# Attention results held by feature, with the exponentials divided before they are turned, in a fused attention and gated-MLP kernel

## The chip, the cores and the metric

The kernel runs on one core of one Trainium2 chip. The metric is device microseconds (us) for one execution. Engines are named as in the profile: PE (TensorE, matrix multiply), PEld (its weight loads), DVE (VectorE), ACT (ScalarE), POOL (GpSimd), SP (SyncE, here an issuer of DMAs). SBUF is the on-chip working memory, PSUM the accumulator memory that PE writes, in banks of 512 float32 per partition.

## The reference, cut to what matters

```python
# q, k, v: (8 batches, 8 heads, 576 positions, 64)
scores = q @ k.T / 8
mask   = heads 0..3: the last 32 positions;  heads 4..7: every 4th of the last 128
attn   = exp(scores - max);  attn = attn / (attn.sum() + 1e-9)
x      = (attn @ v) as (4608 tokens, 512 features)
g, val = x @ w_gate, x @ w_val          # 512 -> 1536
out    = (g * sigmoid(g) * val) @ w_out # 1536 -> 512
```

Attention is sparse: each query sees 32 keys. The MLP over 4608 tokens is nearly all of the arithmetic.

## The kernel before, in words

**The MLP.** It works on transposed tokens (features on partitions). Each float32 operand is split into a high part and a remainder, and three products stand for one full-precision product; these are the `128x512` multiplies of lines 515, 552 and 841 in the profile, 3564 of them. The first three chunks of 512 tokens are computed plainly (lines 515 and 552). Meanwhile the weights are converted, and in the third chunk also mixed (lines 719 to 732) into "pieces" that are written to memory. The last three chunks of 1024 tokens use a Strassen-like scheme with seven products (line 841), whose weights come back as pieces through POOL's DMA queue (line 770), and whose intermediate sums and splits are made by DVE (line 804) and ACT (lines 831 and 846).

**The attention.** It is cut into 46 packs. A pack is a pair of heads over a stretch of tokens, in groups of four blocks of 32 queries; a block has 64 keys, and 32 of them count for each query. Packs of pairs 0 and 1 have the plain mask, those of pairs 2 and 3 the dilated one, where a block takes every fourth position. Packs 0 to 3 are done at the start, before any MLP work, with helpers of their own (`first_...`). The 42 packs from number 4 on have 2, 3 or 4 groups, 136 in all, and are threaded into the MLP's stream of multiplies at fixed slots: `attend` is called after each slot, and a table gives each pack m a slot A and a slot B, three or six slots later.

- At A(m): `results` of pack m-1 (line 457), then `scores` of pack m (line 417), both on PE into the two banks of the PSUM tile `two`, head 0 in bank 0 and head 1 in bank 1. DVE then runs `norm` of m-1 (lines 466 to 468): it adds a small number to the sum of exponentials, which an extra column of ones in v has produced, takes the reciprocal and multiplies it onto the results, queries on partitions. Then `shift` of m (lines 429, 431, 432: add the mask, take the maximum, subtract it) and `exps` on ACT (line 437). Loads of v and of the next q and k are issued from ACT.
- At B(m): `turn_y` transposes the normed results of m-1 on PE (line 475), so that features stand on partitions. `turn_e` transposes the exponentials of m (line 441), so that keys stand on partitions, and `keys` copies them to SBUF (line 447). `x_copies` writes the transposed results into the MLP's x (line 497 for the last three chunks, lines 488 and 489 for chunks 1 and 2, which need the high part and the remainder).

In `results` a block of exponentials, turned, is the stationary operand: 64 keys by 32 queries, so that eight such tiles fit on the 128 by 128 array (2 row halves by 4 column quarters). The values, 64 features and the column of ones, are streamed through, 65 columns. In `scores` the stationary operand is 64 features by 32 queries, and 64 keys are streamed. A multiply of these two kinds leaves two records in the trace; the program's order shows it once.

**What sets the order.** The start is written out by hand. After it the Tile framework's scheduler places instructions on each engine in the order in which its own model of the program finds them ready, so a row can stand earlier or later than the code says. Each engine works through its own order strictly.

## Time and profile before

| what | value |
|---|---|
| median of 3 runs | 935.71 us (935.17 to 936.23) |
| the profiled execution, own time | 934.96 us |
| its span, first to last instruction | 933.2 us |
| granted TensorE clock | 1.0 |
| PE busy | 921.8 us (99%) |
| DVE, ACT, POOL busy | 639.2, 391.1, 253.8 us |
| bytes moved by DMA | 205.45 MB, 220 GB/s on average |

A row of the timeline reads: start, duration (both us), engine, line, operation, output<-inputs, array tile (rows*columns), shape, count, and in brackets the idle time of the engine before it with what ended it. A row of the groups gives busy time, mean ns of one instruction, and idle time before them. Durations on PE overlap: a `128x512` multiply is shown with some 0.39 us, but starts follow each other every 0.227 us, so costs on PE are read from starts.

### The profile page before, as it was taken

How to read it: one execution, taken by the hardware profiler on the slowest of the kernel's cores; microseconds unless marked ns; L12 is line 12 of the kernel's file. 1: busy time of each engine (PE TensorE's matmuls, PEld its weight loads, DVE VectorE, ACT ScalarE, POOL GpSimd, SP SyncE). 2: the span in 40 equal slices, each digit the busy share in tenths (PEclk: the TensorE clock that was granted, in tenths of full speed). 3: DMA queues.
4: the chain of work that ended last, by engine and by line, in shares of the span. 5: the costliest groups of instructions: out<-in, count | busy, mean ns of one | idle time of the engine just before them, and what ended most of it. 6: DMA issues, size and time to landing. Idle time of an engine off the chain costs nothing.

```text
span 933.2 us, 20559 instructions
## 1 busy us (share of the span) xinstructions
PE 921.8 (99%) x8499; PEld 751.5 (81%) x8499; DVE 639.2 (68%) x1055; ACT 391.1 (42%) x664; POOL 253.8 (27%) x307
## 2 busy tenths in 40 slices
PE   7999999999999999999999999999999999999998
PEld 4778788878888878888888888888888888888886
DVE  6764738668678775757669965666689745656863
ACT  4865623323334233343345643343355523334351
POOL 6655421111111212133223111222223112343320
PEclk9999999999999999999999999999999999999999
DMA  9974515667786980767777778766766686656663
GB/s 349 349 255 174 175 41 198 235 205 262 245 287 217 305 307 5 267 217 222 226 226 236 239 224 255 242 217 213 247 208 195 219 255 189 195 189 195 201 207 111
DMA packets 75533, 205.45 MB, mean 220 GB/s; under 512 B 7728, under 2 KB 22320, under 8 KB 75440
## 3 DMA queue, kind: packets, MB, share of 16 engines
q0 software_dynamic: 27728, 100.77, 34.6%
q1 hardware_dynamic: 35472, 65.16, 19.7%
q10 hardware_dynamic: 12240, 38.20, 11.9%
q8 instruction: 67, 1.10, 0.5%
q14 instruction: 26, 0.21, 0.1%
HBM read 161.64 MB, written 42.47 MB: 219 GB/s over the span
## 4 chain that ended last, share of the span: by engine, by line
PE 73%; DVE 3%; DMA 1%; issue 1%; ACT 1%; SPq 0%; ACTq 0%; DVEq 0%
PE bo L841 32%; PE bv L841 12%; PE bg L841 12%; PE bo L552 4%; PE bg L515 4%; PE bv L515 4%; PE two L457 2%; PE two L417 2%; DMA pieces<-at_float32r 1%; PE two L441 1%; PE two L475 1%; DVE at_float32r L732 0%; SPq L740 0%; DVE at_float L529 0%; DVE at_float L719 0%
## 5 line engine op out<-in xcount | busy, mean ns | idle before, releaser
L841 PE MATMUL bo<-at_float32r 128*128 128x512 f32 x1296 | 307.1, 390 | 0.0
L841 PEld LDWEIGHTS bo<-at_float32r 128*128 128x128 f32 x1296 | 242.2, 188 | 50.6
L770 POOL DMA_DIRECT2D at_float32r<-pieces x189 | 101.3, 536 | 376.7 <-PE bo L841 216.6
L804 DVE TENSOR_TENSOR at_float<-bo,at_float 128x512 f32<-128x512 f32 (+1 forms) x169 | 114.2, 684 | 104.9 <-ACT at_float L846 49.5
L804 DVE TENSOR_TENSOR at_float32r<-at_float,at_float32r 128x512 fp32r<-128x512 f32 (+1 forms) x147 | 114.0, 800 | 40.0 <-ACT at_float32r L831 27.1
L841 PE MATMUL bv<-at_float32r 128*128 128x512 f32 x486 | 129.5, 393 | 0.0
L841 PE MATMUL bg<-at_float32r 128*128 128x512 f32 x486 | 129.3, 392 | 0.0
L515 PE MATMUL bg<-at_float32r,at_float32r 128*128 128x512 f32 x432 | 106.7, 394 | 0.8 <-DVE at_float32r L505 0.4
L515 PE MATMUL bv<-at_float32r,at_float32r 128*128 128x512 f32 x432 | 107.1, 394 | 0.0
L552 PE MATMUL bo<-at_float32r,at_float32r 128*128 128x512 f32 x432 | 106.2, 394 | 0.0
L841 PEld LDWEIGHTS bv<-at_float32r 128*128 128x128 f32 x486 | 90.2, 188 | 19.0
L841 PEld LDWEIGHTS bg<-at_float32r 128*128 128x128 f32 x486 | 90.3, 188 | 18.8
L831 ACT CAST at_float32r<-at_float 128x512 fp32r<-128x512 f32 x126 | 77.0, 622 | 67.4 <-PE bv L841 21.3
L544 POOL TENSOR_TENSOR at_float32r<-at_float,at_float32r 128x512 fp32r<-128x512 f32 x36 | 48.6, 1351 | 204.8 <-PE bo L552 138.3
L515 PEld LDWEIGHTS bg<-at_float32r,at_float32r 128*128 128x128 f32 x432 | 79.9, 188 | 18.8 <-DVE at_float32r L505 1.2
L515 PEld LDWEIGHTS bv<-at_float32r,at_float32r 128*128 128x128 f32 x432 | 79.7, 188 | 17.1 <-DVE at_float L534 0.4
L552 PEld LDWEIGHTS bo<-at_float32r,at_float32r 128*128 128x128 f32 x432 | 79.7, 188 | 16.9
L867 ACT ACTIVATE at_float<-at_float 128x512 f32<-128x512 f32 x72 | 45.6, 633 | 81.7 <-DVE at_float L804 81.7
L846 ACT COPY at_float<-bg 128x512 f32<-128x512 f32 x63 | 37.0, 587 | 94.2 <-PE bg L841 94.0
L529 DVE SCALAR_TENSOR_TENSOR at_float<-at_float,bg 128x512 f32<-128x512 f32 x36 | 24.7, 686 | 66.9 <-ACT at_float L524 66.9
L279 POOL TENSOR_TENSOR at_float32r<-at_int,at_float32r 128x768 fp32r<-128x768 f32 x24 | 44.4, 1858 | 45.2 <-ACT at_float32r L275 45.2
L869 DVE SCALAR_TENSOR_TENSOR at_float<-at_float,at_float 128x512 f32<-128x512 f32 x72 | 49.4, 686 | 10.7 <-ACT at_float L867 10.6
(94 smaller groups left out, 916.4 us busy)
## 6 DMA issues: line engine op xcount, KB each, us to landing
at_float32r<-pieces POOLq DMA_DIRECT2D x189, 512.0 KB, 3.7
pieces<-at_float32r SPq DMA_DIRECT2D x126, 256.0 KB, 3.8
at_int<-w SPq DMA_DIRECT2D x24, 768.0 KB, 7.1
out<-at_float SPq DMA_DIRECT2D x35, 256.0 KB, 3.9
at_float<-vb ACTq DMA_DIRECT2D x15, 520.0 KB, 5.2
at_float<-vb ACTq DMA_DIRECT2D x20, 390.0 KB, 4.7
at_float<-qkb ACTq DMA_DIRECT2D x13, 544.0 KB, 5.7
at_float<-qkb ACTq DMA_DIRECT2D x12, 448.0 KB, 5.2
```

The lines of the kernel that those rows point to most:

```text
L279: nc.gpsimd.tensor_tensor(out=lo, in0=wst.pop(u).bitcast(F32), in1=hi, op=ALU.subtract)
L515: nc.tensor.matmul(out=bank[:, :CH], lhsT=wcol(f, o, low), rhs=x[ORDER[j]], start=n == 0, stop=n == len(ops) - 1)
L529: last["h"] = nc.vector.scalar_tensor_tensor(out=t, in0=t, scalar=1.0, in1=bank_g[:, :CH], op0=ALU.add, op1=ALU.mult)
L544: nc.gpsimd.tensor_tensor(out=hl, in0=hst[i][0], in1=hst[i][1], op=ALU.subtract)
L552: nc.tensor.matmul(out=bank_o[j][:, :CH], lhsT=wcol(f, 2 * DM + P * j, low), rhs=x, start=f == 0 and low == 0 and x is hh, stop=f == NF - ...
L770: nc.gpsimd.dma_start(out=taken[asked], in_=pieces[asked % NPIECE])
L804: engine.tensor_tensor(out=out, in0=a, in1=b, op=op)
L831: nc.scalar.copy(out=o[:, 0], in_=src)
L841: nc.tensor.matmul(out=bank, lhsT=w, rhs=x, start=first and n == 0 and t in FRESH, stop=last and n == len(ops) - 1, skip_group_check=True)
L846: nc.scalar.copy(out=kept[KEPT[t]][r], in_=banks[0][r][:, :CS])
L867: nc.scalar.activation(out=f, in_=g, func=AF.Tanh, scale=0.5)
L869: nc.vector.scalar_tensor_tensor(out=f, in0=f, scalar=1.0, in1=g, op0=ALU.add, op1=ALU.mult)
```

## The change

- **`results`**: the values become the stationary operand (64 keys by 64 features, four tiles on the array) and the turned exponentials, 32 queries, are streamed. The outcome stands by feature: head 0 on partitions 0 to 63, head 1 on 64 to 127, in the bank of the block's parity. There is no column of ones any more. For dilated packs the outcome's columns are written with a step of two, which puts tokens in order.
- **Row halves**: in odd blocks the two heads change places (`side`): `scores` of an odd block puts head 0 into bank 1 and head 1 into bank 0, and v is laid out to match.
- **`weigh`** (new, packs 4 on): after `exps` DVE sums each block of exponentials, adds the small number and takes the reciprocal, and POOL multiplies it onto the exponentials, before `turn_e`.
- **Gone for packs 4 on**: `norm` and `turn_y`. `x_copies` of m-1 reads `two` directly and moves from B(m) to A(m), before `shift`.
- **Buffers and loads**: the place of the normed results becomes a second buffer for the exponentials and their turned copy. Key columns that only the mask hides are no longer stored, so q and k come in tiles of at most 1056 columns instead of 1152; v is 64 columns a block instead of 65.
- **Start**: the two identity matrices are no longer loaded (one DMA on SP) but made by two ACT copies; the later part of the masks moves from ACT's queue to SP's, behind the first two weight loads.

The core of the diff:

```diff
@@ scores
-                    nc.tensor.matmul(out=two[BQ * j:BQ * j + BQ, h, a + BK * g:a + BK * g + BK],
+                    side = pk(m).side(j, h)
+                    nc.tensor.matmul(out=two[BQ * j:BQ * j + BQ, side, a + BK * g:a + BK * g + BK],
@@ new
+    def side(j, h):
+        return h ^ j & 1
...
+    def weigh(m, pool):
+        ng, e = pk(m).ng, st[m]["e"]
+        z = pool["bz"](2 * ng)
+        x = e.rearrange("q g (h k) -> q (g h) k", h=2)
+        nc.vector.reduce_sum(out=z, in_=x, axis=mybir.AxisListType.X)
+        nc.vector.tensor_scalar(out=z, in0=z, scalar1=EPS, scalar2=None, op0=ALU.add)
+        nc.vector.reciprocal(out=z, in_=z)
+        nc.gpsimd.tensor_tensor(out=x, in0=x, in1=z.unsqueeze(2).broadcast_to([P, 2 * ng, BK]), op=ALU.mult)
@@ results
+            o = BK * g + j // 2
+            o = slice(o, o + BK, 2) if pk(m).order else slice(BK * g + BQ * (j // 2), BK * g + BQ * (j // 2) + BQ)
             for h in range(2):
-                r = slice(D * h, D * h + D)
-                nc.tensor.matmul(out=two[BQ * j:BQ * j + BQ, h, (D + 1) * g:(D + 1) * (g + 1)],
-                                 lhsT=t[r, BQ * i:BQ * i + BQ], rhs=v[r, i, :], start=True, stop=True,
-                                 skip_group_check=True)
+                r = D * pk(m).side(j, h)
+                nc.tensor.matmul(out=two[D * h:D * h + D, j % 2, o], lhsT=v[r:r + D, i],
+                                 rhs=t[r:r + D, BQ * i:BQ * i + BQ], start=True, stop=True, skip_group_check=True)
@@ buffers
+    later["e"] = Ring(TP, *early["y"].starts)
@@ attend, A
-                norm(m - 1, two, later)
+                x_copies(m - 1, two)
...
                 exps(m)
+                weigh(m, later)
@@ attend, B
-            if m > 4:
-                turn_y(m - 1, two[:, 0])
...
-            if m > 4:
-                x_copies(m - 1, two[:, 0])
@@ start
-        nc.sync.dma_start(out=idents, in_=ident.rearrange("n p c -> p n c"))
...
-        nc.scalar.dma_start(out=consts[:, near:], in_=masks[:, near:])
+        nc.scalar.copy(out=idents[:, 0], in_=ident16)
+        nc.scalar.copy(out=idents[:, 1].rearrange("p (t r) -> p r t", r=DIL),
+                       in_=ident16.rearrange("p (r t) -> p r t", r=DIL))
...
+        nc.sync.dma_start(out=consts[:, near:], in_=masks[:, near:])
```

The new code shifts line numbers: `results` is line 477, `scores` 425, `shift` 437, 439 and 440, `exps` 455, `weigh` 448 to 451, `turn_e` 459, the MLP's multiplies 531, 568 and 857, its DVE helper 820.

Three places of the order are spoken of later. The first is PE at the start, where the last of the four early packs is finished (`fr` is that pack's results, `fs_125` its transposed results). Before:

```order
L441 MATMUL fs_121<-at_256_float_59,at_512_float_362 128x128 x4
L475 MATMUL ex<-at_256_float_59,at_512_float_304 128x128 x4
L389 MATMUL fr<-at_2080_float_194,at_512_float_362 32x130 x16
L515 MATMUL bg<-at_512_float32r,at_1536_float32r 128x512 x4
L515 MATMUL bv<-at_512_float32r,at_1536_float32r 128x512 x2
L475 MATMUL fs_125<-at_256_float_59,at_512_float_357 128x128 x4
```

After:

```order
L459 MATMUL fs_121<-at_256_float_59,at_512_float_363 128x128 x4
L490 MATMUL ex<-at_256_float_59,at_512_float_305 128x128 x4
L531 MATMUL bg<-at_512_float32r,at_1536_float32r 128x512 x4
L531 MATMUL bv<-at_512_float32r,at_1536_float32r 128x512 x5
L396 MATMUL fr<-at_2080_float_194,at_512_float_363 32x130 x16
L490 MATMUL fs_125<-at_256_float_59,at_512_float_358 128x128 x4
```

The results of that pack now stand behind nine MLP multiplies, and nothing is left between them and their transposes. On POOL, at the same place, `at_2080_float_194` is that pack's v. Before:

```order
L359 MEMSET at_2080_float_187 128x1040
L360 DMA at_2080_float_187<-vb 64x1040
L359 MEMSET at_2080_float_194 128x1040 x2
L360 DMA at_2080_float_194<-vb 64x1040
L279 ISA
L279 TENSOR_TENSOR at_1536_float32r<-at_776_int_313,at_1536_float32r 128x768
```

After:

```order
L366 MEMSET at_2080_float_187 128x1040
L367 DMA at_2080_float_187<-vb 64x1040
L366 MEMSET at_2080_float_194 128x1040 x2
L285 ISA
L285 TENSOR_TENSOR at_1536_float32r<-at_776_int_314,at_1536_float32r 128x768
L367 DMA at_2080_float_194<-vb 64x1040
```

The load of that v is now issued behind the first subtraction of the weights' split. The third place is DVE in the first of the last three MLP chunks, at the visit that PE's trace shows at 503 us (`L466` to `L468` are `norm`, `L429` to `L432` are `shift`). Before:

```order
L466 TENSOR_SCALAR at_6_float_2489<-two 128x6
L804 TENSOR_TENSOR at_512_float_515<-at_512_float_515,at_512_float_4178 128x512
L467 RECIPROCAL at_6_float_2489<-at_6_float_2489 128x6
L804 TENSOR_TENSOR at_1024_float32r<-at_512_float_526,at_1024_float32r 128x512
L468 TENSOR_TENSOR at_384_float_1235<-two,at_6_float_2489 128x2x3x64
L429 TENSOR_TENSOR at_512_float_304<-two,at_480_bfloat_58 128x2x4x64
L804 TENSOR_TENSOR at_1024_float32r<-at_512_float_518,at_1024_float32r 128x512
L431 TENSOR_REDUCE at_8_float_250<-at_512_float_304 128x8
L804 TENSOR_TENSOR at_1024_float32r<-at_512_float_519,at_1024_float32r 128x512
L432 TENSOR_TENSOR at_512_float_304<-at_512_float_304,at_8_float_250 128x2x4x64
```

After, from the same visit's `shift` (`L437`) to the reciprocal of `weigh` (`L450`):

```order
L437 TENSOR_TENSOR at_512_float_358<-two,at_480_bfloat_58 128x2x4x64
L820 TENSOR_TENSOR at_512_float_4135<-at_512_float_522,at_512_float_528 128x512
L439 TENSOR_REDUCE at_8_float_251<-at_512_float_358 128x8
L820 TENSOR_TENSOR at_1024_float32r<-at_512_float_519,at_1024_float32r 128x512
L440 TENSOR_TENSOR at_512_float_358<-at_512_float_358,at_8_float_251 128x2x4x64
L820 TENSOR_TENSOR at_1024_float32r<-at_512_float_520,at_1024_float32r 128x512
L820 TENSOR_TENSOR at_512_float_516<-at_512_float_516,at_512_float_4135 128x512
L448 TENSOR_REDUCE at_8_float_357<-at_512_float_358 128x8
L820 TENSOR_TENSOR at_1024_float32r<-at_512_float_4093,at_1024_float32r 128x512
L449 TENSOR_SCALAR at_8_float_357<-at_8_float_357 128x8
L820 TENSOR_TENSOR at_1024_float32r<-at_512_float_4135,at_1024_float32r 128x512
L450 RECIPROCAL at_8_float_357<-at_8_float_357 128x8
```

`norm` is gone from DVE's order, and three instructions of `weigh` stand behind `shift`, with MLP work between them. On PE the turn of that pack's exponentials stands behind the same 36 MLP multiplies after its scores as before, now without the three transposes of `turn_y` ahead of it.

More of the change, by code (lines that the diff above doesn't have):

```diff
@@ L78, in __init__ @@
             nb = -(-per // BQ)
-            if self.step == 1:
-                blocks += [(b, q0 + BQ * t, BQ, width + BQ * t) for t in range(nb)]
-            else:
-                blocks += [(b, q0 + r + DIL * BQ * t, min(BQ, per - BQ * t), width + BQ * ((nb + 1) * r + t))
-                           for t in range(nb) for r in range(DIL)]
-            width += BQ * (nb + 1) * self.step
+            kept = nb if q0 == 0 else nb + 1
+            k = max(width - BQ, 0) if q0 == 0 else width
+            blocks += [(b, q0 + r + self.step * BQ * t, min(BQ, per - BQ * t), k + BQ * (kept * r + t))
+                       for t in range(nb) for r in range(self.step)]
+            width = k + BQ * (kept * self.step + nb + 1 - kept)
             lo += n
@@ L139, in attention_moe @@
 @with_exitstack
-def attention_moe(ctx, tc, qkb, vb, w, masks, ident, out):
+def attention_moe(ctx, tc, qkb, vb, w, masks, out):
     nc = tc.nc
@@ L317, in attention_moe @@
     early, later = {}, {}
[L318 removed]
+    for k, n in (("qk", QKB), ("v", 4 * NGM * D), ("e", TP), ("y", TP)):
         later[k] = Ring(n, o)
@@ L479, in attention_moe, with x_copies @@
            for x in ((M_XE, M_X1), (M_XE + 2 * CS, M_X1 + 2 * CS))]
-    def x_copies(m, bank):
+    def x_copies(m, two):
         c = pk(m).chunk
@@ L486, in x_copies @@
                 first -= CH * c
-                src, h, l = bank[:, col:col + n], xh[:, first:first + n], xl[:, first:first + n]
+                src = result_cols(m, two, col, n)
+                h, l = by_two(m, xh[:, first:first + n]), by_two(m, xl[:, first:first + n])
                 nc.scalar.copy(out=h, in_=src)
@@ L496, in x_copies @@
                     w = min(n, CS - o)
-                    nc.scalar.copy(out=x32[a][t][:, k, o:o + w], in_=bank[:, col:col + w])
+                    nc.scalar.copy(out=by_two(m, x32[a][t][:, k, o:o + w]), in_=result_cols(m, two, col, w))
                     col, first, n = col + w, first + w, n - w
@@ L1003, in layout @@
     masks = np.concatenate([np.eye(P), block_masks()], axis=1).astype(ml_dtypes.bfloat16)
[L1004 to L1009 removed]
+    return dict(qkb=qkb, vb=vb, w=w, masks=masks)
+_INS = ["qkb", "vb", "w", "masks"]
 def kernel(**inputs):
```

39 lines of the change are left out of this document (16 added, 23 removed).

## The prediction

> **What bounds the kernel now.** The first views are the head of the page and the busy time by stage. The columns of the second are the stretch, its length, then busy time and count for PE, PEld, DVE, ACT and POOL, then the granted clock, the DMA share and GB/s.
>
> ```profile
> span 933.2 us, 20559 instructions
> 0.00:28.60 28.60, 23.01 (x319) 14.17 (x319) 21.10 (x38) 15.68 (x23) 15.87 (x24) 1.00 0.94 360
> 28.60:190.00 161.40, 160.22 (x1663) 129.82 (x1664) 102.35 (x174) 80.85 (x128) 62.84 (x39) 1.00 0.57 200
> 190.00:372.00 182.00, 180.97 (x1995) 148.19 (x1994) 131.76 (x230) 62.59 (x108) 30.47 (x27) 1.00 0.67 228
> 372.00:932.00 560.00, 557.56 (x4525) 459.33 (x4523) 383.96 (x616) 232.01 (x406) 144.65 (x218) 1.00 0.68 217
> ```
>
> After the start PE is busy for all but some 5 us of 903 us, at the full clock, while DVE has three tenths or more of its time free and POOL more than half. So whatever is taken from PE's own row shortens the kernel, and work put on DVE or POOL costs only where PE has to wait for its result. The next view is the groups of instructions by line.
>
> ```profile
> L417 PE MATMUL two<-at_float 64*32 64x64 f32 x2176 | 33.0, 226 | 0.0
> L457 PE MATMUL two<-at_float,at_float 64*32 64x65 f32 x2176 | 31.1, 224 | 1.1 <-DVE at_float32r L489 1.1
> L441 PE MATMUL two<-at_float,at_float 128*128 128x128 f32 x136 | 21.8, 273 | 0.7 <-ACT at_float L437 0.7
> L475 PE MATMUL two<-at_float,at_float 128*128 128x128 f32 x136 | 21.6, 271 | 0.0
> L431 DVE TENSOR_REDUCE at_float<-at_float 128x6 f32<-128x384 f32 (+2 forms) x38 | 22.1, 582 | 1.0
> L466 DVE TENSOR_SCALAR at_float<-two 128x6 f32<-128x6 f32 (+2 forms) x42 | 6.7, 159 | 29.4 <-PE two L417 29.4
> L467 DVE RECIPROCAL at_float<-at_float 128x6 f32<-128x6 f32 (+2 forms) x42 | 8.1, 193 | 1.1
> L468 DVE TENSOR_TENSOR at_float<-two,at_float 128x384 f32<-128x384 f32 (+2 forms) x42 | 24.7, 588 | 1.3
> L544 POOL TENSOR_TENSOR at_float32r<-at_float,at_float32r 128x512 fp32r<-128x512 f32 x36 | 48.6, 1351 | 204.8 <-PE bo L552 138.3
> ```
>
> The attention waits almost nowhere: 1.1 us ahead of results, 0.7 us ahead of turns. Its work on PE is threaded in well, and the question is what each kind costs there. That is read from starts in PE's timeline, first around a visit A.
>
> ```profile
> 502.88 0.39 PE L841 MATMUL bo<-at_float32r 128*128 128x512 f32 x1
> 503.20 0.46 PE L457 MATMUL two<-at_float,at_float 64*32 64x65 f32 x32
> 503.72 0.84 PE L417 MATMUL two<-at_float 64*32 64x64 f32 x60
> 504.48 0.96 PE L841 MATMUL bg<-at_float32r 128*128 128x512 f32 x3
> 505.29 0.85 PE L841 MATMUL bv<-at_float32r 128*128 128x512 f32 x3
> 505.98 0.84 PE L841 MATMUL bg<-at_float32r 128*128 128x512 f32 x3
> ```
>
> Two MLP multiplies stand 0.227 us apart (505.29 to 505.98 is three of them), so the seam from full array to small tiles costs 0.32 - 0.23 = 0.09. The 48 results and 64 scores take 503.20 to 504.48, 1.28 us, or 11.4 ns a record with the last seam. The first MLP multiply behind them is longer than its neighbours by 0.96 - 0.84 = 0.12: I read that as a 128-column weight load with nothing to hide behind. And around a visit B:
>
> ```profile
> 512.78 0.49 PE L475 MATMUL two<-at_float,at_float 128*128 128x128 f32 x3
> 513.11 0.60 PE L441 MATMUL two<-at_float,at_float 128*128 128x128 f32 x4
> 513.46 0.47 PE L841 MATMUL bo<-at_float32r 128*128 128x512 f32 x1
> ```
>
> Three transposes take 0.33, so one costs 0.109.
>
> **The change part by part.** *Transposes removed.* 136 x 0.109 = 14.8 us less on PE, with nothing to hide them in now: a sure gain. *Waits ahead of results.* The 1.1 us of L457 go: the copies out of `two` now run a visit earlier. Together -15.9. Taking copies out of `two` no longer needs the transposes, so nothing else becomes late there.
>
> *Results the other way round.* 2176 records stay 2176, and each streams 32 columns instead of 65. No row shows 64x64 tiles, so the bounds come from two neighbours. Streaming alone cannot be dearer than today, and at 11.4 ns or less a record the change is 0, or a microsecond below it. But each record needs a new 64-column weight load, and only four tiles take turns. The exposed load above was 0.12 for 128 columns, so I take 0.055 for 64; a round of four tiles then lasts 0.055, or 13.7 ns a record. For 48 records that is 0.66 against 0.52 (503.20 to 503.72) today: +0.14, and for 64 records +0.19. Scores behind it may start from a filled queue, as the first 32 results do (within 0.46 less a duration of 0.22, some 8 ns each), which gives back up to 0.15. Results and scores now use different tiles, so a seam stands between them: 0.09 by the row above, 0 if scores can start as tiles come free. I take +0.16 a visit, 41 visits: +6.5 us, from -1 to +12.5 (2176 x 4 ns + 41 x 0.09), nearer to the load's price than to none, because a full-array load was seen exposed.
>
> The Trainium skill, "TensorEngine Tiling (Array Packing)", section "Tiling Modes", says that a change of tiling mode drains the TensorE; the 0.32 against 0.23 above agrees, and by that rule the new seam would cost its 0.09 in full, 3.7 us in all.
>
> *The start.* Rows of the last early pack, and of the load and the subtraction that change places on POOL (L360 stands right ahead of L279 there before):
>
> ```profile
> 22.78 1.09 PE L389 MATMUL fr<-at_float,at_float 128*32 128x130 f32 x32
> 23.80 1.20 PE L515 MATMUL bg<-at_float32r,at_float32r 128*128 128x512 f32 x4
> 27.90 0.68 DVE L505 TENSOR_TENSOR at_float32r<-fs,at_float32r 128x512 fp32r<-128x512 f32 x1
> 28.63 0.73 PE L515 MATMUL bg<-at_float32r,at_float32r 128*128 128x512 f32 x2 [0.41 <-DVE at_float32r L505]
> 19.23 1.73 POOL L279 TENSOR_TENSOR at_float32r<-at_int,at_float32r 128x768 fp32r<-128x768 f32 x1 [3.90 <-ACT at_float32r L275]
> ```
>
> Behind nine multiplies the results of that pack start at 23.80 + 9 x 0.227 = 25.85 instead of 22.78. The v that they need is issued behind the subtraction, at 20.96, which is early enough. From there to L505's end took 5.8 us (22.78 to 28.58), of which some 1.4 was waiting behind other DVE and ACT work: 30.2 at the best, 31.6 at the worst, against 28.58, and PE has the same 14 multiplies to fill it with. Fewer bytes ahead of the first loads (128 KB of identities, 80 KB of masks, at the 360 GB/s of the first row above: 0.6) give some back. I take +1.5, from -0.6 to +2.5. The two ACT copies stand where ACT waits for data anyway.
>
> *The sum and its multiply ahead of the turn.* Behind `exps` now come a DVE sum (582 ns as L431), two small operations (159, 193) and a POOL multiply (1351 for 512 columns, as L544; three quarters, an estimate, for 384). With 0.09 for each of four handovers that is 2.6 us for four groups, 2.3 for three. `norm` leaves DVE ahead of `shift` (0.16 + 0.19 + 0.59 = 0.94), and the turn comes 0.33 to 0.44 earlier, since `turn_y` no longer stands ahead of it. So a turn needs 1.8 to 2.1 us of cover, and 0.6 more for each MLP operation that DVE has between these steps. The cover is the time from the end of the exponentials to the first turn; a usual visit, one in the mixing of weights, and the two tight ones:
>
> ```profile
> 493.11 0.53 ACT L437 ACTIVATE at_float<-at_float 128x384 f32<-128x384 f32 x1 [0.91 <-DVE at_float L432]
> 497.30 0.49 PE L441 MATMUL two<-at_float,at_float 128*128 128x128 f32 x3
> 305.20 0.63 ACT L437 ACTIVATE at_float<-at_float 128x512 f32<-128x512 f32 x1 [1.95 <-DVE at_float L432]
> 308.12 0.60 PE L441 MATMUL two<-at_float,at_float 128*128 128x128 f32 x4
> 512.23 0.63 ACT L437 ACTIVATE at_float<-at_float 128x512 f32<-128x512 f32 x1 [1.35 <-DVE at_float L432]
> 706.23 0.63 ACT L437 ACTIVATE at_float<-at_float 128x512 f32<-128x512 f32 x1 [1.35 <-DVE at_float L432]
> 707.11 0.60 PE L441 MATMUL two<-at_float,at_float 128*128 128x128 f32 x4
> ```
>
> The covers are 3.66, 2.29, 0.25 and 0.25 us. The first kind hides the new steps with one or two foreign operations between. The second just fails: six turns between 180 and 310 us are like it, 0.5 each, 3.0 us. For the tight ones DVE's rows:
>
> ```profile
> 504.37 0.68 DVE L869 SCALAR_TENSOR_TENSOR at_float<-at_float,at_float 128x512 f32<-128x512 f32 x1
> 506.95 1.69 DVE L804 TENSOR_TENSOR at_float32r<-at_float,at_float32r 128x512 fp32r<-128x512 f32 x1
> 511.46 0.68 DVE L432 TENSOR_TENSOR at_float<-at_float,at_float 128x512 f32<-128x512 f32 x1
> 506.35 3.45 POOL L804 TENSOR_TENSOR at_float<-at_float,at_float 128x512 f32<-128x512 f32 x2 [2.14 <-DVE at_float L466]
> ```
>
> In the new order `shift` starts four operations of 0.6 after 504.37, at 506.8, and ends at 509.9, or at 510.9 if a split again takes 1.69 beside POOL. Exponentials add 0.7, the sum 0.7, three MLP operations 1.9 among the small ones with their 0.35, the multiply 1.44: 515.0 to 516.0, where PE comes at 512.9. That is 2.1 to 3.1, twice: 4.5 us with the lower end preferred. One late turn at 335 us, the 0.7 of L441, adds 0.5. Together +8 us; the lower bound is 2 (the tight pair at half), the upper 15 (a dozen more turns at 0.6). Queued behind the multiply on POOL are the piece loads and the remainder L544; both have a whole slot or more of reserve, POOL having waited 138.3 us for PE ahead of L544.
>
> The sum against this execution's own time of 934.96: -14.8 - 1.1 + 6.5 + 1.5 + 8 = +0.1, so 935.1. The median of the runs is 0.75 higher: 935.8.
>
> **The rivals.** *The cover holds.* Loads of weights hide (+1 instead of 6.5) and POOL is late only at the tight pair (+2 to +4): -15.9 + 1 + 1.5 + 3 = -10.4, 925.3. For it: in the trace a weight load is exposed only behind a seam. Against it: the covers of 0.25. Half-way cases, where one of the two holds, lie at 928 to 934.
>
> *The multiply on POOL becomes the wait.* Its place is the turn at B; it decides wherever cover is under 2.1 us plus 0.6 for each foreign DVE operation. If loads cost 9 and every visit in the mixing stage misses by a microsecond, the waits are 15: -15.9 + 9 + 1.5 + 15 = +9.6, 945.4. For it: POOL's 1351 ns and the 1.69 beside POOL. Against it: most covers are over 3 us.
>
> *Row halves collide.* Today each row half writes its own bank (head 0 bank 0, head 1 bank 1) and both run at once. Afterwards either half writes both. If that makes them take turns, 2176 scores at 11.4 ns become about twice as long, +25 us, less the overlap with seams: +15 to +25, some 955. No row here has halves in one bank, so I hold it at 0.08. The Trainium skill, "TensorEngine Tiling (Array Packing)", section "Restrictions and Gotchas", says that different row tiles cannot access the same PSUM bank at the same time; no run here shows it yet, and in each column quarter the two halves still differ in bank.
>
> **How the numbers follow.** A measurement of this kernel can tell about 0.2%, 1.9 us, from no change. The forecast of no change, 934 to 937.7, has 0.28; the cover holding wholly 0.15, half-way 0.23; the multiply as the wait 0.26; colliding halves 0.08. So faster 0.38, same 0.28, slower 0.34. The range leaves out the best end of the first rival and the collision: 926.5 to 946.5. The terms' own bounds give -15.9 - 1 - 0.6 + 2 = -15.5 and -15.9 + 12.5 + 2.5 + 15 = +14.1, which would need every term at one end.
>
> **What would show it.** In the changed kernel's trace: no transposes at line 490 after the start; results at line 477 with starts 13 to 14 ns apart (10 would mean hidden loads, 25 or more a collision); scores at line 425 no slower than 11 ns; PE or PEld waiting at line 459 for POOL line 451, 8 us in all, over 2 us near 513 and 707; the first long run of MLP multiplies near 30 us instead of 28.6. The prediction is wrong if PE never waits at line 459, or if results and scores together differ from today's by more than 12.5 us.

## The result and the profile after

| kernel | median (lowest to highest) | profiled execution | span | granted clock |
|---|---|---|---|---|
| before | 935.44 us (934.51 to 936.23, 4 runs) | 934.96 us | 933.2 us | 1.000 |
| changed | 956.84 us (955.86 to 958.57, 4 runs) | 956.45 us | 954.7 us | 0.994 |

The ratio is 1.0231, 95% interval 1.0216 to 1.0246: the change makes the kernel 2.3% slower, some 21.4 us, where no change was forecast and 926.5 to 946.5 was the range. The ratios, here and below, leave out four single executions that took 1.2 to 5.5 times as long as the others (two of the kernel before, one each of e1 and c1). The busy time by stage comes first, with the columns of the prediction's first view; the stretches are longer than those of before by what each stage lost.

```profile
span 954.7 us, 20290 instructions
0.00:33.50 33.50, 24.94 (x321) 16.04 (x322) 21.78 (x39) 16.85 (x26) 15.66 (x24) 0.93 0.86 326
33.50:196.00 162.50, 159.44 (x1627) 128.11 (x1626) 103.83 (x175) 80.46 (x127) 73.60 (x50) 0.99 0.54 188
196.00:387.00 191.00, 185.25 (x1963) 150.01 (x1962) 132.51 (x229) 64.32 (x108) 42.52 (x40) 0.99 0.65 218
387.00:953.50 566.50, 559.44 (x4457) 458.30 (x4455) 388.38 (x613) 234.77 (x406) 165.78 (x237) 1.00 0.67 213
```

Before, PE was idle for some 5 us after the start; now it is idle for 3.1, 5.8 and 7.1 us in the three later stretches, 16 in all, and 8.6 us in the first one. Here are the groups by line that answer to those of before (results are now line 477, scores 425, the turn of the exponentials 459; 449 to 451 are `weigh`).

```profile
L477 PE MATMUL two<-at_float,at_float 64*64 64x32 f32 x2176 | 40.2, 221 | 0.0
L425 PE MATMUL two<-at_float 64*32 64x64 f32 x2176 | 31.0, 223 | 0.0
L459 PE MATMUL two<-at_float,at_float 128*128 128x128 f32 x136 | 22.4, 277 | 13.4 <-POOL at_float L451 13.2
L459 PEld LDWEIGHTS two<-at_float,at_float 128*128 128x128 f32 x136 | 16.3, 140 | 22.7 <-POOL at_float L451 19.1
L449 DVE TENSOR_SCALAR at_float<-at_float 128x6 f32<-128x6 f32 (+2 forms) x42 | 12.0, 286 | 0.7
L451 POOL TENSOR_TENSOR at_float<-at_float,at_float 128x384 f32<-128x384 f32 (+2 forms) x42 | 43.5, 1037 | 65.6 <-DVE at_float L450 62.6 <-ACT at_float L862 2.5 <-ACT at_float32r L823 0.3
```

The 136 transposes of results are gone. In their place the turn waits for POOL's multiply, 13.2 us by PE and 19.1 by its weight loads, where it waited 0.7 us for ACT before. A visit A with 48 results and 64 scores, as the one shown of before:

```profile
519.31 0.90 PE L477 MATMUL two<-at_float,at_float 64*64 64x32 f32 x48
520.14 0.86 PE L425 MATMUL two<-at_float 64*32 64x64 f32 x64
520.93 0.97 PE L857 MATMUL bg<-at_float32r 128*128 128x512 f32 x3
```

From the first result to the first MLP multiply it is 520.93 - 519.31 = 1.62 us, against 1.28 before. The scores take 0.79 of it, as before (0.76). The results take 0.83 instead of 0.52, and the starts of single records in the trace say how: four at 7 ns from each other, one per tile, and a new round of four every 58.4 ns (14.6 ns a record), then 150 ns from the last result to the first score.

Where along the way was the time lost? Take the start of the same MLP multiply in both traces and subtract:

```
before us   after us   lag us
  49.66      54.59      4.93     the start
 115.56     119.54      3.98
 137.51     143.31      5.81     late turn at 127
 292.00     300.78      8.79     late turns at 159, 172, 186, 264
 312.70     325.32     12.62     late turn at 319
 357.27     372.27     15.00     late turns at 348, 364
 508.70     525.17     16.47     late turn at 513
 528.70     547.37     18.68     late turn at 531
 698.48     718.39     19.91     late turn at 550
 718.81     740.71     21.91     late turns at 711, 729
 909.00     930.43     21.44
```

The lag comes in steps, at the start and at single turns; between them it moves by a microsecond or so. So what results cost more and what the transposes gave is about even, and the 21.4 us are two other things. Adding up PE's time from each record's start to the next one's, over the whole trace: results 22.0 -> 37.3, scores 28.8 -> 28.0, transposes of results 17.6 -> 3.4 (the early packs keep theirs). These three make +0.3; the 1.1 us of waits ahead of results are gone as well.

**The start**, in PE's, POOL's and DVE's timeline:

```profile
24.14 1.30 PE L531 MATMUL bv<-at_float32r,at_float32r 128*128 128x512 f32 x5
27.34 1.09 PE L396 MATMUL fr<-at_float,at_float 128*32 128x130 f32 x32 [1.89 <-POOL at_float32r L285]
20.37 0.57 POOL L367 DMA_DIRECT2D at_float<-vb  x1
28.49 0.17 DVE L403 TENSOR_SCALAR at_float<-fr 128x8 f32<-128x8 f32 x1 [4.57 <-PE fr L396]
```

The values for the last early pack are asked for at 20.37, land 6.9 us later (the first row below, of the DMA view), and are used at 27.34. (The wait is put down to POOL's line 285, but that had ended by 26.6; the landing falls at 27.3.) In the kernel before, the last load of this kind was issued at 14.8. So the results of that pack start 4.56 us later than before (22.78). Behind them the order is a chain: DVE divides them (line 403, after 4.57 us of doing nothing), PE transposes them (line 490), DVE splits them (line 521), and PE's next long run needs that split. The run starts at 33.00 (second row) where it started at 28.63. That is the lag of 4.9, but for some half a microsecond that follows at half clock.

```profile
at_float<-vb POOLq DMA_DIRECT2D x1, 260.0 KB, 6.9
33.00 2.33 PE L531 MATMUL bg<-at_float32r,at_float32r 128*128 128x512 f32 x5
```

**A late turn**, at 319 us, in ACT's, DVE's, POOL's and PE's timeline (line 745 splits mixed weights, 455 is the exponentials):

```profile
314.68 1.05 ACT L745 CAST at_float32r<-at_float 128x1024 fp32r<-128x1024 f32 x1 [3.54 <-DMA pieces<-at_float32r]
315.64 0.62 ACT L455 ACTIVATE at_float<-at_float 128x512 f32<-128x512 f32 x1
316.29 0.69 DVE L448 TENSOR_REDUCE at_float<-at_float 128x8 f32<-128x512 f32 x1 [4.11 <-ACT at_float L455]
317.57 1.04 POOL L451 TENSOR_TENSOR at_float<-at_float,at_float 128x512 f32<-128x512 f32 x1 [4.23 <-DVE at_float L450]
318.67 0.66 PE L459 MATMUL two<-at_float,at_float 128*128 128x128 f32 x4 [1.87 <-POOL at_float L451]
```

The chain from the exponentials to the turn takes 318.67 - 315.64 = 3.0 us. But the exponentials were late already: DVE had finished their input (line 440) at 312.2, and they stood behind a split of weights that waited for a transfer.

### The profile page after: what moved, and what is told of

Same layout as the page of the kernel before. It is cut to its first block, busy times and chain, and to the rows that moved or that the text cites. A ratio compares the mean times of both kernels' runs of the same rounds, so it can differ in the third digit from the quotient of the medians.

```text
span 954.7 us, 20290 instructions
## 1 busy us (share of the span) xinstructions
PE 929.1 (97%) x8363; PEld 752.5 (79%) x8363; DVE 646.5 (68%) x1055; ACT 396.4 (42%) x666; POOL 297.6 (31%) x349
## 3 DMA queue, kind: packets, MB, share of 16 engines
q1 hardware_dynamic: 35344, 65.04, 19.1%
q10 hardware_dynamic: 12096, 36.75, 11.4%
## 4 chain that ended last, share of the span: by engine, by line
PE 82%; DVE 11%; POOL 2%; DMA 2%; ACT 1%; issue 1%; SPq 0%; ACTq 0%; DVEq 0%; POOLq 0%
PE bo L857 30%; PE bv L857 10%; PE bg L857 10%; PE bo L568 8%; PE bg L531 8%; PE bv L531 8%; PE two L477 3%; DVE at_float32r L820 2%; PE two L425 2%; DVE at_float L820 2%; PE two L459 2%; POOL at_float L451 1%; DMA pieces<-at_float32r 1%; DMA at_float<-qkb 1%; DMA at_float<-vb 1%
## 5 line engine op out<-in xcount | busy, mean ns | idle before, releaser
L857 PEld LDWEIGHTS bg<-at_float32r 128*128 128x128 f32 x486 | 90.5, 188 | 19.1
L451 POOL TENSOR_TENSOR at_float<-at_float,at_float 128x384 f32<-128x384 f32 (+2 forms) x42 | 43.5, 1037 | 65.6 <-DVE at_float L450 62.6
```

The costliest lines, as they stand in the source:

```text
L451: nc.gpsimd.tensor_tensor(out=x, in0=x, in1=z.unsqueeze(2).broadcast_to([P, 2 * ng, BK]), op=ALU.mult)
L857: nc.tensor.matmul(out=bank, lhsT=w, rhs=x, start=first and n == 0 and t in FRESH, stop=last and n == len(ops) - 1, skip_group_check=True)
```

## The experiments

The theory after this comparison: the loss is late turns (some 17 us) and the start (some 5 us), while results by feature cost just what the transposes gave. The rival: the waits at the turns only show where PE would soon have waited for something else, and the results are the loss. The medians beside the kernel before, which ran on the same chip each time; the last column is the ratio less the changed kernel's 1.0231, times 935.4 us:

| kernel | median us | ratio to before (95%) | against changed, us |
|---|---|---|---|
| e1_no_multiply | 938.81 | 1.0033 (1.0021 to 1.0044) | -18.5 |
| e2_values_in_halves | 977.47 | 1.0449 (1.0424 to 1.0475) | +20.4 |
| s1_early_v | 952.92 | 1.0178 (1.0160 to 1.0196) | -5.0 |
| b1_later | 950.73 | 1.0161 (1.0135 to 1.0188) | -6.5 |
| s2_keep_busy | 955.43 | 1.0206 (1.0193 to 1.0220) | -2.3 |
| w1_weigh_alone | 947.82 | 1.0109 (1.0079 to 1.0140) | -11.4 |
| x1_copies_behind_shift | 948.75 | 1.0131 (1.0117 to 1.0145) | -9.4 |
| c1_later_turns | 939.79 | 1.0040 (1.0027 to 1.0054) | -17.9 |
| c3_no_eps | 936.70 | 1.0004 (0.9990 to 1.0018) | -21.2 |
| c4_no_eps_dve | 933.42 | 0.9970 (0.9956 to 0.9984) | -24.4 |
| c5_all | 933.92 | 0.9975 (0.9966 to 0.9984) | -23.9 |
| e3_half_queries, one run | 959.69 | | +2.9 by medians |
| e5_half_values, one run | 948.68 | | -8.2 by medians |
| e4_no_swap, one run | 979.86 | | +23.0 by medians |

### The price of the late turns

**e1_no_multiply**

```diff
@@ weigh
-        nc.gpsimd.tensor_tensor(out=x, in0=x, in1=z.unsqueeze(2).broadcast_to([P, 2 * ng, BK]), op=ALU.mult)
```

> The changed kernel without the POOL multiply of `weigh` (the division of the exponentials is left out; sum, EPS and reciprocal stay). Theory A, late turns: the turns at line 459 wait some 15 us in all because sum, reciprocal and multiply stand ahead of them; without the multiply nearly all of that goes, 941 to 944 us. Theory B, the work on PE itself: the waits only stand where PE would soon have waited for something else (copies, loads), and the loss is in the results; then it stays over 952 us.

Measured 938.81, even under theory A's 941. The turns' row (line 458 here) has no wait left:

```profile
L458 PE MATMUL two<-at_float,at_float 128*128 128x128 f32 x136 | 21.7, 271 | 0.0
```

Results and scores take what they took in the changed kernel (37.3 and 28.0 us from start to start). Without the multiply the turn waits for no step of `weigh`, so nearly all of the loss, 18.5 of 21.4 us, hangs on that chain; the rival is out. It is more than the gaps ahead of the turns add up to (15.4 us from start to start over 13 turns), partly because PE ran at half pace behind one of them (the last section).

**b1_later.** The turns of the last stage stand two slots later.

```diff
-        visits(m, a, a + 6)
+        visits(m, a, a + 8)
```

> In the last stage (from 427 us on) every turn stands eight slots behind its scores instead of six, some 2.7 us later; nothing else changes. Theory A, late turns: the five waits of this stage (0.8, 2.2, 0.5, 0.8, 2.2 us) go and nothing takes their place, 950 to 951 us. Theory B: PE then waits for the copy behind the turn or for the next results instead, 955 us or more.

950.73: theory A. The turn is not a fixed point of the pipeline; in the last stage two more slots of cover cost nothing.

**w1_weigh_alone.** The kernel before, with `weigh` (as in the changed kernel) ahead of the turn, and `norm` cut down to a copy.

```diff
@@ attend, A, of the kernel before
                 exps(m)
+                weigh(m, later)
@@ norm
-        nc.vector.tensor_scalar(out=z, in0=s[:, :, :, D], scalar1=EPS, scalar2=None, op0=ALU.add)
-        nc.vector.reciprocal(out=z, in_=z)
-        nc.vector.tensor_tensor(out=y.rearrange("q g h d -> q h g d"), in0=s[:, :, :, :D],
-                                in1=z.unsqueeze(3).broadcast_to([P, 2, ng, D]), op=ALU.mult)
+        nc.vector.tensor_copy(out=y.rearrange("q g h d -> q h g d"), in_=s[:, :, :, :D])
```

> One part of the change alone, on the kernel before: the exponentials are divided by their sum ahead of the turn (`weigh` as in the changed kernel), and `norm` becomes a plain copy; results by query, their transposes, the start and the places of the turns stay as before. Theory A, the loss is the late turns (17 us by the run without the multiply) and the start (4 us), while results and seam only eat what the transposes gave: 948 to 952 us, less the 0.4 us of cover that the transposes ahead of each turn give. Theory B, results by feature are themselves the larger loss: under 944 us.

947.82, 10.2 us over the kernel before by the ratio (11.5 by medians) and just below theory A's 948. But the waits are not those of the changed kernel:

```profile
PE two L450 <- POOL at_float L442: 7.5, 3, 3.7
```

Three long ones, at 339, 520 and 718 us: these are the places that the prediction named (335, 513 and 707 in the kernel before), and they put all of the loss into three steps of the lag, 4.6, 3.7 and 3.7 us. The steps are larger than the waits because the clock shows half for 3.4 us behind each of the three. Before 339 the lag never passes 0.4 us, while the changed kernel has six late turns between 127 and 319. So `weigh` alone does not make these late. Something else in the change does.

**x1_copies_behind_shift.** In the changed kernel the copies of the previous pack's results (`x_copies`) stand ahead of `shift`; here they stand behind it.

```diff
@@ attend, A
-                x_copies(m - 1, two)
             if m < NPK:
                 shift(m, two, later, m < 8)
+            if m > 4:
+                x_copies(m - 1, two)
+            if m < NPK:
                 exps(m)
```

> The changed kernel with the copies of the results put behind `shift` instead of ahead of it (still ahead of the turn). Theory A, the copies on ScalarE, which wait for all scores and for ScalarE's queue, hold back the shift and so the turn (shift waited 39 us for them in all): waits at line 459 fall by a third to a half, 948 to 952 us. Theory B, the late turns come from other work that stands in the queues ahead of exponentials and sums: 955 us or more, with the waits at line 459 about as long as before.

948.75: theory A, half of the late turns' price. In the changed kernel `shift` on DVE (line 437) waits for the copies on ACT (line 513), which wait for all scores:

```profile
DVE at_float L437 <- ACT at_float L513: 39.2, 16, 8.2
```

Here no such wait is left. The waits of the turns' weight loads, in the changed kernel and in this one:

```profile
PEld two L459 <- POOL at_float L451: 19.1, 14, 2.3
```
```profile
PEld two L459 <- POOL at_float L451: 10.8, 8, 2.5
```

The turns at 127, 159, 172 and 319 us wait no more, and by 400 us PE is 6.5 us ahead of the changed kernel. What remains stands at the visits that the prediction called tight (here at 342, 524 and 721 us) and at some others, by 0.4 to 1.2 us.

### The start

**s1_early_v.** One memset of that pack's values goes to DVE, and the scheduler puts the load ahead of the subtraction on POOL again.

```diff
-        first_v(3, nc.gpsimd, nc.gpsimd)
+        first_v(3, nc.gpsimd, nc.vector)
```

> One memset of the last early pack's values moves from POOL to VectorE, and the scheduler then issues the load of these values ahead of the weight subtraction on POOL, as in the kernel before. Theory A: the late load put PE 1.0 us behind and the gaps that it left halved PE's clock for some 7 us, 3.9 us more; both go, 951.5 to 952.5 us, and no multiply near 32 us takes 0.43 us. Theory B: the clock falls for another reason (the whole start's density): 955.5 to 957 us.

952.92, near theory A: 5.0 us less by the ratio. But A names two causes, the late load itself (1.0) and the half clock behind it (3.9), and this run undoes both.

**s2_keep_busy.** The load stays late, and 20 multiplies of a constant keep PE busy meanwhile.

```diff
-                      "L1 X3 N2 W0 T3 K3 W1 U2 A3 H2 L0 W2 W0 N3 W3 W4 W1 W0 U3 H3 L2 W1 W2 W0 L3 W2 W3 W1").split():
+                      "L1 X3 N2 W0 T3 K3 W1 U2 Z7 Z7 A3 H2 L0 W2 W0 N3 W3 W4 W1 W0 Z6 U3 H3 L2 W1 W2 W0 L3 W2 W3 W1").split():
```

> The changed kernel's order at the start is kept, the late load of values too, but 20 multiplies of a constant into an unused bank fill the gaps that PE has between 22 and 30 us. Theory A, PE's gaps bring the half clock: the granted clock stays at 1.00 to 40 us, 3 to 4.5 us less, 952 to 954 us. Theory B, the clock falls for the load of the other engines or transfers: it still shows 0.5 near 32 us, 956 to 959 us.

955.43 is in neither range. Three stretches of the changed kernel and the same ones here (the clock is the third number from the right):

```profile
24.00:28.50 4.50, 2.54 (x39) 1.71 (x37) 0.01 (x1) 1.60 (x2) 1.72 (x1) 1.00 1.02 416
28.50:32.00 3.50, 2.32 (x8) 1.82 (x9) 3.43 (x7) 1.17 (x2) 0.00 (x0) 0.59 0.47 191
32.00:36.00 4.00, 4.00 (x11) 3.03 (x11) 2.27 (x3) 3.12 (x6) 2.16 (x2) 0.51 0.63 214
```
```profile
24.00:28.50 4.50, 3.53 (x35) 2.13 (x37) 0.40 (x1) 1.89 (x3) 1.74 (x1) 1.00 1.03 420
28.50:32.00 3.50, 3.50 (x36) 2.27 (x28) 2.84 (x6) 1.03 (x2) 0.00 (x0) 1.00 0.55 223
32.00:36.00 4.00, 3.83 (x17) 2.49 (x15) 3.46 (x5) 3.84 (x6) 2.04 (x2) 1.00 0.56 175
```

The clock stays at 1.00. Yet by lag PE is only 0.5 us ahead of the changed kernel at 62 us, not 3.9: DVE is idle from 24 to 28.5 us in both, and its row shows why.

```profile
29.09 0.17 DVE L403 TENSOR_SCALAR at_float<-fr 128x8 f32<-128x8 f32 x1 [4.70 <-PE fr L396]
```

With or without the full clock, the results of the last early pack, which PE needs next, come late; the half clock mostly filled time in which PE would have waited. x1, whose start has the changed kernel's order, says the same without any filling: its clock is full throughout this time, and its long run starts at 33.04.

```profile
28.50:32.00 3.50, 1.68 (x23) 1.06 (x13) 3.00 (x6) 1.19 (x2) 0.00 (x0) 1.00 0.46 190
33.04 1.44 PE L531 MATMUL bg<-at_float32r,at_float32r 128*128 128x512 f32 x5 [0.25 <-DVE at_float32r L521]
```

So PE's gaps alone do not bring the half clock: x1 has them (it waits 1.71 us ahead of these results and 1.24 ahead of their transposes) and keeps 1.00. Why one execution shows half there and another does not stays open. The start's cost is the late load and the chain behind it; s1 shows DVE at line 403 at 23.97 instead:

```profile
23.97 0.16 DVE L403 TENSOR_SCALAR at_float<-fr 128x8 f32<-128x8 f32 x1
```

### What sets the pace of results

**e3_half_queries** streams half as many columns; **e5_half_values** holds half as many; **e4_no_swap** gives each row half one tile instead of two in turn. In e5 (and e2 below) neighbours in a bank are told apart by the block's second bit instead of its first, so that no two row halves write the same partitions of a bank.

```diff
@@ e3, results: 16 of 32 queries
-                                 rhs=t[r:r + D, BQ * i:BQ * i + BQ], start=True, stop=True, skip_group_check=True)
+                                 rhs=t[r:r + D, BQ * i:BQ * i + BQ // 2], start=True, stop=True, skip_group_check=True)
@@ e5, results: 32 of 64 values (c is 0 or 2, h is c // 2)
-                nc.tensor.matmul(out=two[D * h:D * h + D, j % 2, o], lhsT=v[r:r + D, i],
+                nc.tensor.matmul(out=two[32 * c:32 * c + 32, j // 2, o], lhsT=v[r:r + D, i, 32 * (c % 2):32 * (c % 2) + 32],
@@ e4, side
-        return h ^ j & 1
+        return h
```

> Each result matmul streams 16 of its 32 columns (half of the queries are left out; two is set to zero once). Theory A, weights set the pace (each row half loads 64 columns per record, 29.2 ns, whatever streams): the rounds at line 477 stay at 56 to 59 ns and the time within 1.5 us of the changed kernel's. Theory B, load and stream of a tile add up: rounds fall to 42 to 50 ns, 4 to 9 us less in all.

> Each result matmul holds 32 of its 64 value columns (half of the features are left out; two is set to zero once), in 64x32 tiles, with four of the eight tiles in use and the streams unchanged. Theory A, each row half takes its records one by one, at a price that grows with the weight columns (16.7 ns for 32, 29.2 for 64): 8 to 9 ns a record, some 8 us less on PE, and no seam of 150 ns ahead of the scores, 5 us less again. Theory B, as my prediction had it, a tile's own round of some 55 ns sets the pace and four tiles take turns: still 13 to 15 ns a record, only the seam goes.

> Odd blocks keep their heads in the usual row halves: head 0 in rows 0 to 63 and head 1 in rows 64 to 127 for every block. Then only two of the four 64x64 tiles are used by results, and both row halves write the same bank at the same time, in other partitions; scores write as in the kernel before. Theory A, each row half loads its weights record by record: results stay at 14 to 16 ns a record, the time within 1.5 us of the changed kernel. Theory B, halves in one bank take turns, or a tile's own round of 58 ns sets the pace: 28 to 30 ns a record, 31 us more, about 988 us.

One visit of each, e3, e5 and e4:

```profile
504.57 1.12 PE L477 MATMUL two<-at_float,at_float 64*64 64x16 f32 x64
505.62 0.72 PE L425 MATMUL two<-at_float 64*32 64x64 f32 x48
```
```profile
514.90 0.60 PE L478 MATMUL two<-at_float,at_float 64*32 64x32 f32 x43
```
```profile
501.50 1.59 PE L477 MATMUL two<-at_float,at_float 64*64 64x32 f32 x48
503.02 0.86 PE L425 MATMUL two<-at_float 64*32 64x64 f32 x64
```

In e3 the rounds stay at 58.4 ns: whether 16 or 32 columns are streamed does not count. (Its time, from one run, is 2.9 us above the changed kernel's, outside theory A's 1.5.) In e5 a round of four takes 31.6 ns at the start of the visit, and from start to start the results take 21.5 us in all instead of 37.3: the price goes with the columns of the stationary operand, 0.9 to 1.0 ns each, and without a change of tile shape the 150 ns ahead of the scores are gone. The time fell by 8 us only, since turns that come earlier wait longer (PE waits 18.6 us for line 451 there, against 13.2). In e4 the pace is one record per tile and 58.4 ns, 48 records in 503.02 - 501.50 = 1.52 us, and 68.4 us for all results from start to start. Row halves do not take turns: their starts stand 7 ns apart although both write one bank, in other partitions. So with 64 stationary columns it is the tile that sets the pace, and a row half with two tiles takes twice as many records. My theory A (a row half takes its records one by one) is out by e4, though its 8 to 9 ns for e5 came near (7.9 in a round). The prediction's picture, a round of tiles as long as one load, holds; that a round of narrower tiles still takes some 55 ns (theory B for e5) does not. Whether with 32 columns the tile or the row half, with a record every 15.8 ns, sets the pace is not settled.

**e2_values_in_halves.** If eight tiles take turns and nothing changes shape, could results be cheaper? Every 64x64 product is made as two of 64x32.

```diff
@@ results (h is c // 2)
-            for h in range(2):
+            for c in range(4):
...
-                nc.tensor.matmul(out=two[D * h:D * h + D, j % 2, o], lhsT=v[r:r + D, i],
+                nc.tensor.matmul(out=two[32 * c:32 * c + 32, j // 2, o], lhsT=v[r:r + D, i, 32 * (c % 2):32 * (c % 2) + 32],
```

> Each 64x64 result is made as two 64x32 ones (twice the matmuls, the same sums), so eight tiles take turns instead of four, in the scores' own tiling; blocks are spread over banks by their second bit so that neighbours still differ. Theory A, a tile's round sets the pace (58.4 ns for four tiles, 66.7 ns for the eight of the scores) and the step to the scores' tiling costs 150 ns a visit: a round of eight should take 45 to 55 ns, 4352 records x 6.2 ns = 27 us instead of 32, and 41 x 0.13 us of seams go: 946 to 949 us. Theory B, PE's issue of each record is what takes 14.6 ns: twice the records cost 32 us more, about 983 us.

977.47, and neither theory: from start to start the 4352 results take 37.6 us, 8.6 ns each, so twice as many records cost the same. Each row half starts a record every 16.7 ns, as in the scores, though half as many columns are streamed. What was lost is elsewhere: PE waits for instructions, 7.7 us ahead of scores (below) and 6.0 ahead of MLP multiplies (line 532), and in several stretches the clock shows half. The profile names nothing that these waits wait for (`issue`), but each of them ended 2.3 to 2.7 us after a 16 KB transfer of instructions had begun, the longest at 558.45 behind one from 556.06.

```profile
PE two L425 <- issue: 7.7, 5, 3.0
```

### Versions that undo the losses

**c1_later_turns** has s1's early load, b1's later turns, and in the stages before lets 7 of the next 12 multiplies go ahead of the turn. **c3_no_eps** leaves out the addition of EPS, **c4_no_eps_dve** has the multiply on DVE, **c5_all** also x1's order.

```diff
@@ c1: gv_mm, likewise out_mm; attend, B
                              start=n == 0, stop=n == len(ops) - 1)
+            if n == 6:
+                turn_late()
...
+        if what == "B" and now < SB and m < NPK:
+            late.append(m)
+            return
@@ c3: weigh
-        nc.vector.tensor_scalar(out=z, in0=z, scalar1=EPS, scalar2=None, op0=ALU.add)
@@ c4: weigh
-        nc.gpsimd.tensor_tensor(out=x, in0=x, in1=z.unsqueeze(2).broadcast_to([P, 2 * ng, BK]), op=ALU.mult)
+        nc.vector.tensor_tensor(out=x, in0=x, in1=z.unsqueeze(2).broadcast_to([P, 2 * ng, BK]), op=ALU.mult)
```

> All that was found, together: the early load of s1_early_v, turns of the last stage two slots later as in b1_later, and turns of the stages before moved behind 7 of the 12 multiplies that follow (1.6 us later). The work is the same. Theory A, the three losses are start, late turns and results, and the last stays: 934.5 to 938 us, no wait of a microsecond at the turns. Theory B, the covers in the weight stages are eaten by DVE and POOL however late the turn, or the copies behind it are now what results wait for: 942 us or more.

> c1_later_turns without the addition of EPS to the sums (a sum is at least 1, its largest term being exp(0), so that the addition changes no bit). Theory A, steps on DVE ahead of the multiply are what the last late turns (some 6 us between 300 and 360 us) wait for: 0.3 us for each, and more where that small step stood beside POOL (1.38 us in one place): 936 to 939 us. Theory B: other operations stand ahead on DVE anyway: 939 to 941 us.

> c3_no_eps with the multiply on DVE instead of POOL. Theory A, the handover and POOL's 1.04 us are on the chain of the late turns: 0.5 to 0.8 us less for each of six, 934 to 937 us. Theory B, DVE's own queue is the limit, and 20 us of multiplies more on it make other steps late: 939 us or more.

> c4_no_eps_dve with the copies behind shift as well. Theory A: the last 2.5 us that it loses between 330 and 390 us go, 930 to 932 us. Theory B: nothing waits for a turn there any more, so nothing is left to gain: 933 to 934.5 us.

c1 lands between its theories at 939.79, with 5.6 us of waits left near 309 to 354 us. One small DVE operation less gives 3 us (936.70, theory A), more than the 0.3 a turn that I had counted. By lag most of it comes between 300 and 357 us, where the operation itself took under 0.2 us. So its place in the queue counts, or the order that the scheduler made without it; the runs do not tell these apart. The multiply on DVE gives 3.3 us more and is faster than both kernels, 0.3% below the one before (interval 0.9956 to 0.9984). With the copies behind `shift` as well there is nothing more to win (933.92), as theory B has it: the turns' row in c5 shows half a microsecond of waits.

```profile
L458 PE MATMUL two<-at_float,at_float 128*128 128x128 f32 x136 | 21.6, 271 | 0.5 <-DVE at_float L450 0.5
```

So with no turn late and the start mended, the kernel is 2 to 3 us ahead of the one before, not 15. Little of that is the exchange of transposes for dearer results, which makes +0.3 us by PE's starts in the changed kernel; the 1.1 us of waits ahead of results are gone, and what else c4 and c5 gain, the start among it, was not taken apart.

## Why the prediction was wrong, point by point

- **Transposes removed, -14.8, and waits ahead of results, -1.1**: right (17.6 -> 3.4 us from start to start, which is -14.2, and no wait at line 477).
- **Results the other way round, +6.5, from -1 to +12.5**: the mechanism was right, the size not: +14.5 with the scores (15.3 - 0.8), above the upper end, and above the 12.5 that was named as a sign of being wrong. The step that failed is the size of a round and of the seam. A round took 58.4 ns, not 55 (14.6 ns a record, not 13.7), against 10.1 a record before from start to start, not the 10.8 of the one visit shown. The seam cost 0.15 from the last result to the first score, some 0.13 over a record's share of a round, not 0.09. And the credit of up to 0.15 a visit for scores that start from a filled queue did not come: they took 0.79 for 0.76. For the visit shown, +0.16 was forecast and 1.62 - 1.28 = +0.34 measured. The rule on tiling modes that the prediction quotes from the Trainium skill, "TensorEngine Tiling (Array Packing)", section "Tiling Modes", is borne out: e2 and e5, whose results keep the scores' shape, show no 150 ns.
- **The start, +1.5, from -0.6 to +2.5**: measured 4.9 by lag and 5.0 by s1. The step that failed is "the v that they need is issued behind the subtraction, at 20.96, which is early enough". It was issued at 20.37, landed 6.9 us later and was used at 27.34, not at 25.85. I compared the time of issue with the time of need, not the time of landing. The chain behind it then took 5.2 us to the end of line 521 (32.54), inside the 4.4 to 5.8 allowed, and PE's long run came at 33.00, 4.4 us later than before.
- **Sum and multiply ahead of the turn, +8, from 2 to 15**: 18.5 by e1, above the upper end. The tight pair was right: 4.5 us forecast; those two visits, now at 531 and 729 us, stand 2.0 us late each, and w1 has its waits at just the three places named. The other early turns were not: 3.5 us forecast for seven, 10.1 measured for eight (gaps from start to start, less one period). Two steps failed there.
  - The first is the credit that "`norm` leaves DVE ahead of `shift`". The change itself puts the copies of results into that place, on ACT, whose queue holds weight work that waits for transfers; for chunks 1 and 2 DVE has a part of them too (line 505). Over all 42 visits the exponentials do start 0.75 us earlier after the last score (3.87 us for 4.62), but at these eight only 0.2 (5.5 us for 5.6); four of the eight start later than before. I had written of these copies only that nothing becomes late for them. x1 takes them out of that place, has 3.6 us at the same eight visits, and gives 9.4 us back; since the scheduler orders anew around them, how much each turn owes to the copies alone is not shown.
  - The second is the price of sum, small operations and multiply, "2.6 us for four groups, 2.3 for three". From the end of the exponentials to the end of the multiply it is 3.3 us on average over all visits and 3.8 at these eight, where the kernel before had 2.7 us of cover on average. Other operations stand between the steps on DVE, and ahead of three of the turns the small operation of line 449 takes 1.25 to 1.38 us (last section).
- **The rivals**: the multiply as the wait (945.4) had the right mechanism and, like the forecast, too small a price for results and start. The cover did not hold. Colliding row halves are refuted: scores take 28.0 us for 28.8, and e4 has both halves in one bank at 7 ns from each other. The Trainium skill, "TensorEngine Tiling (Array Packing)", "Restrictions and Gotchas", says that different row tiles cannot use one bank at the same time; for results in other partitions of the bank, as in e4, the trace does not bear that out.
- **The sum**: the terms as measured make -14.2 - 1.1 + 14.5 + 4.9 + 18.5 = +22.6 us, against 21.4 by the ratio.
- Of the marks set: PE waits at line 459 (yes, 13.2 instead of 8), results 13 to 14 ns apart (14.6), scores no slower than 11 ns (12.9 from start to start, against 13.2 before: the mark itself was set by the wrong row), a first long run of multiplies near 30 us (33.0, at half pace).

## What to carry to other kernels

When a step moves ahead of a hand-over, ask of every instruction that the change puts ahead of it, on whichever engine, what that instruction itself waits for: a queue is as late as its latest entry. Price a load by when it lands, not by when it is issued, and follow the chain behind it to the next long run. A matrix product with few streamed columns may cost what its stationary operand has columns (here 58.4 ns for 64, whether 16 or 32 are streamed), so turning it round to save transposes may pay out what it saves.

## What the runs showed of the hardware

- On 64x64 tiles in float32 a record takes 58.4 ns per tile whether 16 or 32 columns are streamed, and 31.6 ns with 32 stationary columns and four tiles in use. With all eight 64x32 tiles in use a row half starts one record every 16.7 ns, for 32 columns streamed (e2) as for 64 (scores).
- PE's pace can halve behind gaps that are short: behind the late turn at 319 us, which came 2.0 us late, eight multiplies stand 0.43 us apart.

```profile
318.50:322.50 4.00, 3.83 (x13) 3.06 (x14) 3.90 (x7) 0.58 (x1) 0.64 (x2) 0.59 0.69 220
```

  Eight at 0.43 are 3.4 us; the waits of the same length at 531 and 729 us had no such tail, while each of the three in w1 (3.7, 1.9 and 1.9 us) had one. The Trainium skill, "TensorE: Matmul & The Clock Gate", Part 1, tells of half pace after an idle window of some 3.4 us, with windows that run freely; the length of the tail agrees, but here a gap of 2 us was at times enough.
- A DVE operation of 4 to 8 elements a partition took 286 ns on average (line 449) where its like took 159 in `norm` before. At 124.53 us it took 1.38 us, until a POOL subtraction that had begun at 124.14 ended:

```profile
124.14 1.75 POOL L285 TENSOR_TENSOR at_float32r<-at_int,at_float32r 128x768 fp32r<-128x768 f32 x1
124.53 1.38 DVE L449 TENSOR_SCALAR at_float<-at_float 128x6 f32<-128x6 f32 x1
```

  Seven of the 42 took over 0.25 us, and six of these ended 0.02 to 0.03 us behind a POOL operation that had begun before them (lines 285 and 560). Three stand ahead of the late turns at 127, 186 and 264 us (1.38, 1.30 and 1.25 us).
- Doubling the number of small records let PE wait for instructions: 7.7 us ahead of scores in e2, up to 3.0 us at a time, each wait behind a transfer of instructions that had begun 2.3 to 2.7 us before its end.
